# Decayed linear attention and two gated MLPs on one core: transposing a chunk's q and k together, by 64-row halves of the array

## The chip, the cores and the metric

One core of a Trainium2 chip. The metric is the device time of one execution in microseconds (us), the median over runs. Engine names are those of the profile: PE is the matrix engine, PEld its weight loads, DVE, ACT and POOL the vector, scalar and GpSimd engines, SP the engine that issues the loads.

## What is computed

The reference, cut to what matters. Attention runs over blocks with a state that decays; its output goes through a gated MLP, and that one's output through a second MLP with h·cos(h).

```python
for b in range(nb):                       # q, k, v: (2, 8, 768, 64), blocks of 64
    intra = einsum('bhic,bhjc->bhij', qb, kb) * Dmask
    intra = einsum('bhij,bhjd->bhid', intra, vb)
    inter = einsum('bhid,bhde->bhie', qb * lam_pow, kv_state)
    out[:, :, sl] = intra + inter
    kv_state = lam_block * kv_state + einsum('bhsd,bhse->bhde', kb * rev_pow, vb)
x = out as (1536, 512)
g = x @ w_gate; x = (silu(g) * (x @ w_val)) @ w_out      # inner width 1536
h = x @ w_in;   y = (h * cos(h)) @ w2_out                # inner width 2048
```

## The kernel before

Attention is done in 12 chunks of 128 tokens (6 for each batch), all 8 heads at once, in fp32. A chunk takes these steps on PE; the letters are those of the table `STEPS`, which sets their order by hand:

- `q`, `k` (line 1072): four transposes each, of 128 tokens by two heads (128 columns), into one PSUM bank; `q` against `anti`, which reverses the tokens, `k` against `ident`. ACT copies each bank to SBUF (`t_copy_job`, tiles `qt` and `kt`, 128x512).
- `s` (line 1089): scores, 8 matmuls that each use 64 rows of the array, the two halves writing two banks. DVE multiplies them with the decay mask (`at`).
- `a` (line 1102): scores by `v`, 8 matmuls with 64 output columns each. `c` (line 1111) adds the state's part on four 64x64 quarters. ACT and DVE then split the sum into two parts for the MLP (`xh`, `xl`).
- `d` (line 1096): the state's update from `kd` (made on POOL) and `v`.
- `m`, once: 16 small matmuls that write the mask.
- `u`: one unit of the first MLP, 12 matmuls of 512 columns (lines 154 to 156), put between steps of attention. Units need the outputs of four chunks.

A suffix is the chunk: `a6` is step `a` of chunk 6. An fp32 matmul is two rows of the profile (x16 for 8 matmuls), a transpose is one.

A second table, `LOADS`, sets the order in which SP issues the loads of q, k, v (one of 256 KB per chunk each) and of the first weights (`G0` and so on, two loads each); tiles come from pools of 3, 3 and 5 buffers (`BUFS`). While the program is built, a planner walks both tables with costs per step (`ATT_NS`, `SWITCH`, the landing rules in `qkv_job`), and so fixes the order of all other work: which matmul of the MLPs comes next, the order on ACT, DVE and POOL. Where it reckons that PE would stand idle for over a microsecond in attention, it puts matmuls on zeros there (`zero`, 256 columns of bf16), as many as fill the gap.

When attention is over its tiles are freed (`open_mlp`), and the rest of the program is the two MLPs: 2568 matmuls.

Of the kernel before, what the change touches and what calls it, by code (L numbers as in the profile page):

```python
# [13 lines left out]
ALU = mybir.AluOpType  # L14
# [33 lines left out]
EARLY = 4  # L48
LATENCY = 130
ISSUE = 400  # L50
STALL, FETCHES = 1000, (13300, 20600, 28400, 36000, 44000, 51500, 62500)
BEHIND = 7000
ATT_NS = {"t": 437, "mask": 700, "s": 892, "st": 464, "av": 875, "qs": 440}
TILES = {"mask": "32", "s": "64*128", "st": "128*64", "av": "128*64", "qs": "64*64"}
STEPS = (
# [3 lines left out]
)  # L59
LOADS = (  # L60
    "q0 k0 k1 q1 k2 q2 v0 k3 k4 q3 k6 v1 q4 q5 q6 k5 v2 v3 k7 v4 q7 v5 G0 v6 q8 v7 "
    "k8 v8 q9 k9 q10 q11 k10 V0 k11 v9 v10 v11 G1 V1"
)
HELD = 6, 7, 8, 9
BUFS = {"q": 3, "k": 3, "v": 5, "qt": 2, "kt": 2, "qd": 3, "kd": 2, "at": 2, "stmp": 2}
WARM = 4, 5


# [4 lines left out]
def kernel(  # L73
# [152 lines left out]

    def att_tile(nm, i):

        shape = {"q": [P, H, D], "k": [P, H, D], "v": [P, H, D], "kd": [P, H, D], "at": [P, H, C], "stmp": [P, NPAIR, D]}
        return att.tile(shape.get(nm, [P, NPAIR, C]), F32, tag=f"{nm}{i}", name=nm)  # L230

    def zero(ps, n):
# [52 lines left out]
            xs[nm, blk] = tuple(xp.tile([P, KD, TB], F32R, tag=f"{t}{blk}", name=t) for t in ("xh", "xl"))  # L285
        return xs[nm, blk]

    kinds = {"q": ("t", "q"), "k": ("t", "k"), "m": ("mask",), "s": ("s",), "d": ("st",), "a": ("av",), "c": ("qs",)}
    steps_of = [None if o == "u" else kinds[o[0]] + ((int(o[1:]),) if o[1:] else ()) for o in STEPS.split()]


# [212 lines left out]
    def signal(name, t):  # L504

        when[name] = t
        for job in blocked.pop(name, ()):
            resume(job, t)
# [93 lines left out]

        return "plain2" in when and ("r", 0, "3") not in when

    last_small, last_tiles = [False], [None]

    def switch(sub):

        kind = sub["op"][0]
        return SWITCH.get(kind, 110) if TILES.get(kind) != last_tiles[0] else 0  # L610

    def small(sub):

# [27 lines left out]
    def run_pe(sub, end, idle):  # L641

        unit = any(sub is s for s in pe_units)
        last_small[0] = small(sub)
        last_tiles[0] = TILES.get(sub["op"][0])
        for subs in (pe_att, pe_units, pe_downs):
            subs[:] = [s for s in subs if s is not sub]
        items = []
        for _ in range(int(sub["bank"])):
            item = min(stock["bank"])  # L650
            stock["bank"].remove(item)
            items.append(item[1])
            if unit:
                unit_banks.add(item[1])
        sub["fn"](*(items or [None]), **({"idle": idle} if idle and sub["op"][0] in ATT_NS and items else {}))
        for key in sub["keys"]:
            left[key] -= 1
            if not left[key]:
                give("ring", where.pop(key), end)
                ring_down(end)  # L660
        sub["then"](end + LATENCY)

    def drop_bank(i, t):

        unit_banks.discard(i)
        give("bank", i, t)
# [260 lines left out]
    def qkv_job(nm, g):  # L927

        src = {"q": q, "k": k, "v": v}[nm]
        i = yield "take", nm  # L930
        t = att_tile(nm, i)
        b, c = divmod(g, CPB)
        made_att[nm, g] = i, t
        yield go("SP", 1100, lambda: nc.sync.dma_start(t, src[b, :, c * C:(c + 1) * C, :].rearrange("h p d -> p h d")))  # L934
        signal((nm, g), landing((yield "now",) - LATENCY - 1100 + 3000, 1140))

    def mask_job(got):

# [6 lines left out]
            drop_bank(b, (yield "now",))  # L945
        signal("dmask", (yield "now",))

    def t_copy_job(nm, g, b, ps):

        i = yield "take", nm + "t"  # L950
        t = att_tile(nm + "t", i)
        yield act(t.rearrange("p a i -> p (a i)"), ps, AF.Copy)
        made_att[nm + "t", g] = i, t
        drop_bank(b, (yield "now",))
        signal((nm + "t", g), (yield "now",))
        if nm == "q" and g % CPB:
            yield "wait", "lrow"
            j = yield "take", "qd"
            qd = att_tile("qd", j)
            yield tt(qd[:, :, ::-1], t, lrow, ALU.mult, "POOL")  # L960
            made_att["qd", g] = j, qd
            signal(("qd", g), (yield "now",))
            done("qt", g, (yield "now",))

    def kd_job(g):

# [11 lines left out]
    def done(nm, g, t):  # L978

        n = readers[nm, g] = readers.get((nm, g), 0) + 1  # L980
        if n == (2 if nm in ("k", "v", "qt") and (nm == "qt" and g % CPB or nm != "qt" and g % CPB != CPB - 1) else 1):
            give(nm, made_att.pop((nm, g))[0], t)

    def tmp_job(g):
# [65 lines left out]
    def att_sub(op):  # L1050
# [1 line left out]
        kind, g = op[0], op[-1]  # L1052
        got = []
        needs, n = {
            "t": lambda: ([op[1:]], 1), "mask": lambda: (["skewed"], 4), "s": lambda: ([("qt", g), ("kt", g)], 2),
            "st": lambda: ([("kd", g), ("v", g)], 1), "av": lambda: ([("at", g), ("v", g)], 2),
            "qs": lambda: ([("av", g), ("state", g), ("qd", g)], 0),
        }[kind]()
# [5 lines left out]
        def fn(*bs, idle=0):  # L1064
            got.extend((b, bank_tile(b)) for b in bs if b is not None)
            if got:
                ps = got[0][1]
                zero(ps, idle)
            if kind == "t":
                src = made_att[op[1], g][1]  # L1070
                for p in range(NPAIR):
                    nc.tensor.transpose(  # L1072
                        ps[:, p * P:(p + 1) * P], src[:, 2 * p:2 * p + 2, :].rearrange("p a d -> p (a d)"),
                        anti if op[1] == "q" else ident,
                    )
            elif kind == "mask":
                for a in range(P // QB):
                    for r, (_, ps) in enumerate(got):
                        rows = slice(QB * r, QB * r + QB)
                        nc.tensor.matmul(  # L1080
                            ps[QB * a:QB * a + QB, 0:2 * C].rearrange("p (g x) -> p g x", g=2), ident[rows, rows],
                            skewed[1][rows, :, QB * a:QB * a + C], start=True, stop=True, tile_position=(QB * r, QB * a),
                        )
            elif kind == "s":
                qt, kt = made_att["qt", g][1], made_att["kt", g][1]
                for p in range(NPAIR):
                    for h2, (_, ps) in enumerate(got):
                        r = slice(64 * h2, 64 * h2 + 64)
                        nc.tensor.matmul(ps[:, p * C:(p + 1) * C], kt[r, p, :], qt[r, p, :], start=True, stop=True)  # L1089
            elif kind == "st":  # L1090
                pv = ps[:, 0:NPAIR * D].rearrange("p (a e) -> p a e", a=NPAIR)
                kd, vn = made_att["kd", g][1], made_att["v", g][1]
                for p in range(NPAIR):
                    for h2 in range(2):
                        h = 2 * p + h2
                        nc.tensor.matmul(pv[64 * h2:64 * h2 + 64, p, :], kd[:, h, :], vn[:, h, :], start=True, stop=True)  # L1096
            elif kind == "av":
                at_, vn = made_att["at", g][1], made_att["v", g][1]
                made_att["out", g] = list(got)
                for f in range(2):  # L1100
                    for a in (0, 2, 1, 3):
                        nc.tensor.matmul(  # L1102
                            put(got, f, a), vn[:, 2 * a + f, :], at_[:, 2 * a + f, :],
                            start=a % 2 == 0, stop=not g % CPB and a % 2 == 1, skip_group_check=True,
                        )
            else:
                out_, qd = made_att["out", g], made_att["qd", g][1]
                for y in range(2):
                    for f, a in ((0, y), (1, y + 2), (0, y + 2), (1, y)):
                        r = slice(64 * f, 64 * f + 64)  # L1110
                        nc.tensor.matmul(  # L1111
                            put(out_, f, a), state[g % 2][r, a, :], qd[r, a, :], start=False, stop=y == 1, skip_group_check=True
                        )

        def then(t):
            if kind == "t":
                spawn(t_copy_job(op[1], g, *got[0]), seen[op] + 1, t)
                done(op[1], g, t)
            elif kind == "mask":
                spawn(mask_job(got), seen[op], t)  # L1120
            elif kind == "s":
                spawn(at_job(g, got), seen[op] + 1, t)
                done("qt", g, t)
                done("kt", g, t)
            elif kind == "st":
                spawn(state_job(g, *got[0]), seen[op], t)
                done("kd", g, t)
# [527 lines left out]
```

## Time and profile before

| | |
|---|---|
| median of 3 runs | 587.58 us (587.55 to 587.71) |
| the profiled execution's own time | 587.25 us |
| its span | 585.5 us |
| PE busy | 579.5 us, 99% of the span |
| DVE, ACT, POOL busy | 504.5, 363.8, 33.4 us |
| chain that ended last | PE 97%, DMA 2% |
| attention on PE | 4.18 to 72.30 us of the span, with six units in it |

The span runs from the first to the last instruction of the program; the execution's own time is 1.75 us longer. An engine's busy share says little where it overlaps with others: what ends the program is read from the chain and from the waits.

### The profile page before, as it was taken

The numbers are of one execution on the slowest core, as the hardware profiler recorded it, in microseconds if no ns is written. First come the engines' busy times: TensorE is split into PE (matmuls) and PEld (weight loads), VectorE is DVE, ScalarE is ACT, GpSimd is POOL, SyncE is SP. The second block draws the span as 40 slices with busy tenths as digits, with TensorE's granted clock in tenths as the row PEclk, the third lists the DMA queues.
The fourth block names the chain that finished last, engine by engine and source line by source line (L and its number), as shares of the span: only waits on it lengthen the run. The fifth ranks groups of instructions, "written<-read, shape, count | busy, mean of one in ns | idle before, by whom it ended". The sixth has DMA issues, their size and how long they took to land.

```text
span 585.5 us, 9450 instructions
## 1 busy us (share of the span) xinstructions
PE 579.5 (99%) x3493; PEld 491.5 (84%) x3493; DVE 504.5 (86%) x943; ACT 363.8 (62%) x689; POOL 33.4 (6%) x50
## 2 busy tenths in 40 slices
PE   8999999999999999999999999999999999999997
PEld 6888788888888888888888888888888888888886
DVE  6479799989698997797889999979898999999973
ACT  4454576777655655465443669886667676867740
POOL 6744000000000000000000000000000000000000
PEclk9999999999999999999999999999999999999999
DMA  9999523546567636426442332111202030300023
GB/s 193 213 202 213 132 61 108 163 145 186 173 195 199 182 108 178 145 90 207 136 137 80 109 125 73 58 51 37 72 32 77 1 112 34 109 0 1 1 86 132
DMA packets 72817, 66.68 MB, mean 114 GB/s; under 512 B 40002, under 2 KB 60738, under 8 KB 72770
## 3 DMA queue, kind: packets, MB, share of 16 engines
q1 hardware_dynamic: 72768, 66.07, 40.9%
q8 instruction: 27, 0.44, 0.3%
q14 instruction: 20, 0.16, 0.1%
q10 hardware_dynamic: 2, 0.00, 0.0%
HBM read 54.00 MB, written 12.06 MB: 113 GB/s over the span
## 4 chain that ended last, share of the span: by engine, by line
PE 97%; DMA 2%; SPq 0%; issue 0%; DVE 0%
PE bank L154 25%; PE bank L155 24%; PE bank L156 24%; PE bank L1485 6%; PE bank L1486 6%; PE bank L1487 6%; PE bank L1089 2%; PE bank L1072 2%; PE bank L1102 2%; DMA v<-in_v_dram 1%; PE bank L1111 1%; DMA q<-in_q_dram 1%; PE bank L1096 1%; SPq L934 0%; DVE sum L529 0%
## 5 line engine op out<-in xcount | busy, mean ns | idle before, releaser
L154 PE MATMUL bank<-xl,wh 128*128 128x512 f32 (+1 forms) x336 | 117.9, 351 | 0.0
L155 PE MATMUL bank<-xh,wh 128*128 128x512 f32 (+1 forms) x336 | 117.4, 350 | 0.0
L156 PE MATMUL bank<-xh,wl 128*128 128x512 f32 (+1 forms) x336 | 117.2, 349 | 0.0
L536 ACT ACTIVATE s<-s 128x512 f32<-128x512 f32 (+2 forms) x124 | 72.9, 593 | 54.0 <-DVE s L529 30.1
L536 ACT ACTIVATE s<-bank 128x512 f32<-128x512 f32 (+2 forms) x126 | 62.8, 501 | 62.7 <-PE bank L156 47.1
L154 PE MATMUL bank<-wl,gh 128*128 128x512 f32 (+1 forms) x196 | 75.6, 386 | 0.0
L155 PE MATMUL bank<-wh,gh 128*128 128x512 f32 (+1 forms) x196 | 75.6, 386 | 0.0
L156 PE MATMUL bank<-wh,gl 128*128 128x512 f32 (+1 forms) x196 | 75.4, 385 | 0.0
L536 ACT ACTIVATE gh<-s 128x512 fp32r<-128x512 f32 x84 | 52.7, 629 | 36.0 <-PE bank L1486 22.3
L529 DVE TENSOR_TENSOR sum<-bank,sum 128x512 f32<-128x512 f32 (+1 forms) x97 | 62.8, 679 | 11.0 <-PE bank L156 8.2
L154 PEld LDWEIGHTS bank<-xl,wh 128*128 128x128 f32 x336 | 63.5, 189 | 9.5 <-issue 0.3
L156 PEld LDWEIGHTS bank<-xh,wl 128*128 128x128 f32 x336 | 63.5, 189 | 8.6 <-DVE wl L541 0.2
L155 PEld LDWEIGHTS bank<-xh,wh 128*128 128x128 f32 x336 | 63.6, 189 | 8.4
L529 DVE TENSOR_TENSOR s<-bank,s 128x512 f32<-128x512 f32 (+1 forms) x102 | 56.8, 561 | 15.3 <-PE bank L156 14.0
L536 ACT ACTIVATE wh<-ct 128x512 fp32r<-128x512 f32 x91 | 55.8, 625 | 17.1 <-DVE ct L205 12.4
L541 DVE TENSOR_TENSOR wl<-ct,wh 128x512 fp32r<-128x512 f32 x91 | 61.7, 685 | 4.1 <-ACT wh L536 3.8
L529 DVE TENSOR_TENSOR gl<-s,gh 128x512 fp32r<-128x512 f32 x84 | 57.4, 686 | 5.2 <-ACT gh L536 4.9
L1486 PE MATMUL bank<-gh,wh 128*128 128x512 f32 x144 | 56.1, 390 | 0.0
L1485 PE MATMUL bank<-gh,wl 128*128 128x512 f32 x144 | 56.1, 390 | 0.0
L1487 PE MATMUL bank<-gl,wh 128*128 128x512 f32 x144 | 56.0, 389 | 0.0
L205 DVE SCALAR_TENSOR_TENSOR ct<-ct,raw 128x512 int32<-128x512 int32 x68 | 48.1, 707 | 2.8 <-ACT ct L193 1.2
L193 ACT ACTIVATE ct<-raw 128x512 f32<-128x512 f32 x68 | 44.5, 662 | 3.8 <-DMA raw<-in_moe_w_in_dram 1.9
(170 smaller groups left out, 1029.8 us busy)
## 6 DMA issues: line engine op xcount, KB each, us to landing
raw<-in_moe_w_out_dram SPq DMA_DIRECT2D x28, 512.0 KB, 3.4
raw<-in_moe_w_in_dram SPq DMA_DIRECT2D x16, 512.0 KB, 3.9
raw<-in_moe_w_gate_dram SPq DMA_DIRECT2D x24, 256.0 KB, 4.7
raw<-in_moe_w_val_dram SPq DMA_DIRECT2D x24, 256.0 KB, 4.2
draftout<-raw SPq DMA_DIRECT2D x9, 512.0 KB, 2.6
q<-in_q_dram SPq DMA_DIRECT2D x12, 256.0 KB, 5.0
k<-in_k_dram SPq DMA_DIRECT2D x12, 256.0 KB, 4.9
v<-in_v_dram SPq DMA_DIRECT2D x12, 256.0 KB, 6.1
```

The lines of the kernel that those rows point to most:

```text
L154: nc.tensor.matmul(ps, wh, xl, start=first, stop=False, **kw)
L155: nc.tensor.matmul(ps, wh, xh, start=False, stop=False, **kw)
L156: nc.tensor.matmul(ps, wl, xh, start=False, stop=last, **kw)
L193: nc.scalar.activation(t, words[:, :, 1].bitcast(F32), AF.Prelu, scale=2.0 ** -112, alpha=2.0 ** 32)
L205: nc.vector.scalar_tensor_tensor(out=w, in0=w, scalar=3, in1=lo, op0=ALU.logical_shift_left, op1=ALU.bitwise_or)
L529: engine, 66 + n * 1.047 if engine == "DVE" else n * 2.45, lambda: unit.tensor_tensor(out=out, in0=in0, in1=in1, op=op),
L536: return go("ACT", (175 if fn == AF.Silu else 40) + n * 0.94, lambda: nc.scalar.activation(out, src, fn, **kw))
L541: return "any", {"DVE": 66 + n * 1.047, "POOL": n * 2.45}, lambda e: (nc.vector if e == "DVE" else nc.gpsimd).tensor_tensor(out=out, in0=i ...
L1072: nc.tensor.transpose(ps[:, p * P:(p + 1) * P], src[:, 2 * p:2 * p + 2, :].rearrange("p a d -> p (a d)"), anti if op[1] == "q" else ident,)
L1485: nc.tensor.matmul(ps, lo[:, cs], gh, start=first, stop=False)
L1486: nc.tensor.matmul(ps, hi[:, cs], gh, start=False, stop=False)
L1487: nc.tensor.matmul(ps, hi[:, cs], gl, start=False, stop=last)
```

## The change

`q` and `k` of a chunk become one step `t`. Each transpose of 128 tokens is cut into two, one for each half of the tokens: 64 rows of the array, 64 columns of `ident` or `anti`, 128 columns of weights. The upper half's results go to one bank and the lower half's to another, q and k side by side in each, so that a step takes two banks. ACT empties them with two copies of 512 columns into one tile `qkt`. The loads are in another order, the steps too, with three units among them in place of six, and the planner's costs are altered.

```diff
-ATT_NS = {"t": 437, "mask": 700, "s": 892, "st": 464, "av": 875, "qs": 440}
+ATT_NS = {"t": 470, "mask": 700, "s": 892, "st": 464, "av": 875, "qs": 440}
-TILES = {"mask": "32", "s": "64*128", "st": "128*64", "av": "128*64", "qs": "64*64"}
+TILES = {"mask": "32", "t": "64*128", "s": "64*128", "st": "128*64", "av": "128*64", "qs": "64*64"}
-    "q0 k0 m q1 k1 s0 s1 q2 k2 a0 q3 s2 a1 d0 d1 a2 c1 k3 k4 q4 c2 d2 s3 s4 q5 q6 "
+    "t0 m s0 t1 a0 t2 s1 d0 s2 d1 a1 t3 t4 a2 s3 d2 c2 c1 d3 a3 d4 c3 t5 s4 t6 s5 "
...
-    "q0 k0 k1 q1 k2 q2 v0 k3 k4 q3 k6 v1 q4 q5 q6 k5 v2 v3 k7 v4 q7 v5 G0 v6 q8 v7 "
+    "q0 k0 k1 q1 q3 k2 q4 q2 k3 q5 v0 k4 k6 k5 v1 v2 q6 k7 v3 v4 G0 v5 k8 q7 v6 q8 "
...
-    def t_copy_job(nm, g, b, ps):
+    def t_copy_job(g, got):
-        i = yield "take", nm + "t"
-        t = att_tile(nm + "t", i)
-        yield act(t.rearrange("p a i -> p (a i)"), ps, AF.Copy)
+        i = yield "take", "qkt"
+        t = att_tile("qkt", i)
+        for r, (b, ps) in enumerate(got):
+            part = t.rearrange("p a n (x i) -> p a (n x) i", x=2)[:, :, 0:4:3] if r else t.rearrange("p a n (x i) -> p a (n x) i", x=2)[:, :, 1:3]
+            yield act(part, ps.rearrange("p (n a i) -> p a n i", n=2, a=NPAIR), AF.Copy)
...
-                src = made_att[op[1], g][1]
-                for p in range(NPAIR):
-                    nc.tensor.transpose(
-                        ps[:, p * P:(p + 1) * P], src[:, 2 * p:2 * p + 2, :].rearrange("p a d -> p (a d)"),
-                        anti if op[1] == "q" else ident,
-                    )
+                for n, nm in enumerate("qk"):
+                    src = made_att[nm, g][1]
+                    for p in range(NPAIR):
+                        for h in range(2):
+                            rows, c = slice(64 * h, 64 * h + 64), h if nm == "k" else 1 - h
+                            nc.tensor.transpose(
+                                got[h][1][:, (n * NPAIR + p) * 64:(n * NPAIR + p) * 64 + 64],
+                                src[rows, 2 * p:2 * p + 2, :].rearrange("p a d -> p (a d)"),
+                                (anti if nm == "q" else ident)[rows, 64 * c:64 * c + 64],
+                            )
```

Three places show how the order moves. The first is PE from the scores of chunk 0 to its step `a0` (`at` by `v`). Before:

```order
L1089 MATMUL bank_254<-qt,kt 128x128
L1089 MATMUL bank_271<-qt,kt 128x128
L1072 MATMUL bank_287<-anti,q 128x128 x4
L1072 MATMUL bank_295<-ident,k 128x128 x4
L1102 MATMUL bank_306<-at,v 64x128 x4
```

Now, one row for each kind of matmul (bank 247 has the scores of chunk 0, banks 262 and 263 the transposes of chunk 1):

```order
L1097 MATMUL bank_247<-qkt 128x128
L1079 MATMUL bank_262<-anti,q 128x64
L1079 MATMUL bank_263<-anti,q 128x64
L1079 MATMUL bank_262<-ident,k 128x64
L234 MATMUL bank_298<-zeros 128x256
L1110 MATMUL bank_298<-at,v 64x128 x4
```

Before, PE has the scores of chunks 0 and 1 and the transposes of chunk 2 behind it when it comes to `a0`; now only the scores of chunk 0 and the transposes of chunk 1. In their place stand 26 matmuls on zeros. Five more stand ahead of the first transposes; before, the planner put none into attention.

The second place is the head of SP's queue. Before, from the fifth load on:

```order
L934 DMA k<-in_k_dram 128x8x64
L934 DMA q<-in_q_dram 128x8x64
L934 DMA v<-in_v_dram 128x8x64
L934 DMA q<-in_q_dram 128x8x64
L934 DMA v<-in_v_dram 128x8x64
```

Now:

```order
L936 DMA k<-in_k_dram 128x8x64
L936 DMA q<-in_q_dram 128x8x64 x2
L936 DMA v<-in_v_dram 128x8x64 x2
L936 DMA q<-in_q_dram 128x8x64
L936 DMA k<-in_k_dram 128x8x64 x2
```

The first `v` was the seventh load and is the eighth; q of chunk 3 goes ahead of it. Further down, v of chunk 6 is the 25th load in both.

The third place is PE around `a6` (bank 786 of the new order has its result). Now:

```order
L1119 MATMUL bank_727<-qd,state_97 64x128
L1079 MATMUL bank_761<-anti,q 128x64
L1079 MATMUL bank_762<-ident,k 128x64
L1110 MATMUL bank_786<-at,v 64x128 x4
L1104 MATMUL bank_805<-v,kd 64x64 x8
L154 MATMUL bank_819<-xl,wh 128x512
L1097 MATMUL bank_857<-qkt 128x128
```

Before, the scores of chunk 7 and the state's update with chunk 6, `s7` and `d6`, stood ahead of `a6`; now both come behind it, `s7` behind the first unit too.

## Rows read from the trace of the kernel before

**Rows 1.** The page's first part: busy time, share of the span, instructions.

```profile
PE 579.5 (99%) x3493; PEld 491.5 (84%) x3493; DVE 504.5 (86%) x943; ACT 363.8 (62%) x689; POOL 33.4 (6%) x50
```

**Rows 2.** Waits of PE over the whole span: us in total, times, longest.

```profile
PE bank L234 <- DVE halfpi L1594: 1.1, 1, 1.1
PE bank L1102 <- DMA v<-in_v_dram: 0.5, 1, 0.5
PE bank L1072 <- DMA q<-in_q_dram: 0.4, 1, 0.4
```

**Rows 3.** Timeline of PE, start of attention: start us, us, matmuls merged.

```profile
11.91 1.09 PE L1102 MATMUL bank<-at,v 128*64 128x128 f32 x16
12.94 0.66 PE L1072 MATMUL bank<-anti,q 128*128 128x128 f32 x4
13.52 1.16 PE L1089 MATMUL bank<-qt,kt 64*128 64x128 f32 x16
```

**Rows 4.** Timeline of PE, further on, for the pace of each step.

```profile
25.07 1.04 PE L1102 MATMUL bank<-at,v 128*64 128x128 f32 x16
25.95 0.63 PE L1096 MATMUL bank<-v,kd 128*64 128x64 f32 x16
26.41 1.04 PE L1102 MATMUL bank<-at,v 128*64 128x128 f32 x16
...
51.49 0.60 PE L1072 MATMUL bank<-anti,q 128*128 128x128 f32 x4
51.93 0.60 PE L1072 MATMUL bank<-ident,k 128*128 128x128 f32 x4
52.46 2.08 PE L1089 MATMUL bank<-qt,kt 64*128 64x128 f32 x32
54.47 0.67 PE L1111 MATMUL bank<-qd,state 64*64 64x128 f32 x16
```

**Rows 5.** Weight loads by form, 10 to 75 us: busy us, mean ns of one.

```profile
L1102 PEld LDWEIGHTS bank<-at,v 128*64 128x64 f32 x192 | 10.3, 137 | 1.8 <-issue 1.5 <-DVE at L529 0.2
L1089 PEld LDWEIGHTS bank<-qt,kt 64*128 64x128 f32 x174 | 10.3, 187 | 0.9 <-issue 0.5 <-ACT kt L536 0.2 <-ACT xh L536 0.2
L1096 PEld LDWEIGHTS bank<-v,kd 128*64 128x64 f32 x160 | 5.6, 137 | 1.1 <-issue 0.9 <-POOL kd L529 0.2
L1072 PEld LDWEIGHTS bank<-ident,k 128*128 128x128 f32 x40 | 4.5, 140 | 0.8 <-issue 0.5
```

**Rows 6.** Timeline of PE from step a6 to the end of attention.

```profile
35.98 1.07 PE L1102 MATMUL bank<-at,v 128*64 128x128 f32 x16
36.98 0.66 PE L1072 MATMUL bank<-anti,q 128*128 128x128 f32 x4
37.57 0.47 PE L154 MATMUL bank<-xl,wh 128*128 128x512 f32 x1
...
40.49 0.60 PE L1072 MATMUL bank<-ident,k 128*128 128x128 f32 x4
...
71.70 0.67 PE L1111 MATMUL bank<-qd,state 64*64 64x128 f32 x16
72.30 0.50 PE L154 MATMUL bank<-xl,wh 128*128 128x512 f32 x1
```

**Rows 7.** The same, in the MLP: the thirteenth matmul after a start at 79.23.

```profile
79.23 0.39 PE L154 MATMUL bank<-xl,wh 128*128 128x512 f32 x1
...
81.95 0.39 PE L154 MATMUL bank<-xl,wh 128*128 128x512 f32 x1
```

**Rows 8.** SP's queue: issue of the seventh load (v0) and the 25th (v6).

```profile
6.12 1.15 SPq L934 DMA_DIRECT2D v<-in_v_dram  x1
...
27.94 1.28 SPq L934 DMA_DIRECT2D v<-in_v_dram  x1
```

**Rows 9.** Issues at 6.12 (at 8.50 alike) and at 27.94: KB, us to landing.

```profile
v<-in_v_dram SPq DMA_DIRECT2D x1, 256.0 KB, 5.1
...
v<-in_v_dram SPq DMA_DIRECT2D x1, 256.0 KB, 7.4
```

More of the change, by code (lines that the diff above doesn't have):

```diff
@@ L50 @@
 ISSUE = 400
-STALL, FETCHES = 1000, (13300, 20600, 28400, 36000, 44000, 51500, 62500)
+STALL, FETCHES = 1000, (13000, 20600, 29000, 36500, 45000, 54500, 63500)
 BEHIND = 7000
-ATT_NS = {"t": 437, "mask": 700, "s": 892, "st": 464, "av": 875, "qs": 440}
-TILES = {"mask": "32", "s": "64*128", "st": "128*64", "av": "128*64", "qs": "64*64"}
+ATT_NS = {"t": 470, "mask": 700, "s": 892, "st": 464, "av": 875, "qs": 440}
+TILES = {"mask": "32", "t": "64*128", "s": "64*128", "st": "128*64", "av": "128*64", "qs": "64*64"}
 STEPS = (
[3 rows of a table removed]
[3 rows of a table added]
 )
 LOADS = (
-    "q0 k0 k1 q1 k2 q2 v0 k3 k4 q3 k6 v1 q4 q5 q6 k5 v2 v3 k7 v4 q7 v5 G0 v6 q8 v7 "
-    "k8 v8 q9 k9 q10 q11 k10 V0 k11 v9 v10 v11 G1 V1"
+    "q0 k0 k1 q1 q3 k2 q4 q2 k3 q5 v0 k4 k6 k5 v1 v2 q6 k7 v3 v4 G0 v5 k8 q7 v6 q8 "
+    "v8 v7 k9 q9 q10 k10 k11 q11 V0 v9 v11 v10 V1 G1"
 )
 HELD = 6, 7, 8, 9
-BUFS = {"q": 3, "k": 3, "v": 5, "qt": 2, "kt": 2, "qd": 3, "kd": 2, "at": 2, "stmp": 2}
+BUFS = {"q": 3, "k": 3, "v": 5, "qkt": 2, "qd": 3, "kd": 2, "at": 2, "stmp": 2}
 WARM = 4, 5
@@ L227, in att_tile @@
     def att_tile(nm, i):
-        shape = {"q": [P, H, D], "k": [P, H, D], "v": [P, H, D], "kd": [P, H, D], "at": [P, H, C], "stmp": [P, NPAIR, D]}
+        shape = {"q": [P, H, D], "k": [P, H, D], "v": [P, H, D], "kd": [P, H, D], "at": [P, H, C], "stmp": [P, NPAIR, D], "qkt": [P, NPAIR, 2, C]}
         return att.tile(shape.get(nm, [P, NPAIR, C]), F32, tag=f"{nm}{i}", name=nm)
@@ L286, in x_tiles @@
         return xs[nm, blk]
-    kinds = {"q": ("t", "q"), "k": ("t", "k"), "m": ("mask",), "s": ("s",), "d": ("st",), "a": ("av",), "c": ("qs",)}
+    kinds = {"t": ("t",), "m": ("mask",), "s": ("s",), "d": ("st",), "a": ("av",), "c": ("qs",)}
     steps_of = [None if o == "u" else kinds[o[0]] + ((int(o[1:]),) if o[1:] else ()) for o in STEPS.split()]
@@ L603, in turning @@
         return "plain2" in when and ("r", 0, "3") not in when
-    last_small, last_tiles = [False], [None]
+    last_small, last_tiles = [False], [None, True]
     def switch(sub):
         kind = sub["op"][0]
-        return SWITCH.get(kind, 110) if TILES.get(kind) != last_tiles[0] else 0
+        if TILES.get(kind) != last_tiles[0]:
+            return SWITCH.get(kind, 145)
+        return 60 if last_tiles[1] and kind not in ATT_NS else 0
     def small(sub):
@@ L644, in run_pe @@
         last_small[0] = small(sub)
-        last_tiles[0] = TILES.get(sub["op"][0])
+        last_tiles[:] = TILES.get(sub["op"][0]), sub["op"][0] in ATT_NS
         for subs in (pe_att, pe_units, pe_downs):
@@ L934, in qkv_job @@
         yield go("SP", 1100, lambda: nc.sync.dma_start(t, src[b, :, c * C:(c + 1) * C, :].rearrange("h p d -> p h d")))
-        signal((nm, g), landing((yield "now",) - LATENCY - 1100 + 3000, 1140))
+        signal((nm, g), landing((yield "now",) - LATENCY - 1100 + 3000, 1200 if landed[0] < 15000 else 1130))
     def mask_job(got):
@@ L946, in mask_job @@
         signal("dmask", (yield "now",))
-    def t_copy_job(nm, g, b, ps):
-        i = yield "take", nm + "t"
-        t = att_tile(nm + "t", i)
-        yield act(t.rearrange("p a i -> p (a i)"), ps, AF.Copy)
[L953 to L956, printed above, removed]
+    def t_copy_job(g, got):
[4 more added lines that the diff above has]
+            yield act(part, ps.rearrange("p (n a i) -> p a n i", n=2, a=NPAIR), AF.Copy)
+            drop_bank(b, (yield "now",))
+        made_att["qkt", g] = i, t
+        signal(("qkt", g), (yield "now",))
+        if g % CPB:
             yield "wait", "lrow"
@@ L959, in t_copy_job @@
             qd = att_tile("qd", j)
-            yield tt(qd[:, :, ::-1], t, lrow, ALU.mult, "POOL")
+            yield tt(qd[:, :, ::-1], t[:, :, 0], lrow, ALU.mult, "POOL")
             made_att["qd", g] = j, qd
             signal(("qd", g), (yield "now",))
-            done("qt", g, (yield "now",))
+            done("qkt", g, (yield "now",))
     def kd_job(g):
@@ L980, in done @@
         n = readers[nm, g] = readers.get((nm, g), 0) + 1
-        if n == (2 if nm in ("k", "v", "qt") and (nm == "qt" and g % CPB or nm != "qt" and g % CPB != CPB - 1) else 1):
+        if n == (2 if nm in ("k", "v", "qkt") and (nm == "qkt" and g % CPB or nm != "qkt" and g % CPB != CPB - 1) else 1):
             give(nm, made_att.pop((nm, g))[0], t)
@@ L1054, in att_sub @@
         needs, n = {
-            "t": lambda: ([op[1:]], 1), "mask": lambda: (["skewed"], 4), "s": lambda: ([("qt", g), ("kt", g)], 2),
+            "t": lambda: ([("q", g), ("k", g)], 2), "mask": lambda: (["skewed"], 4), "s": lambda: ([("qkt", g)], 2),
             "st": lambda: ([("kd", g), ("v", g)], 1), "av": lambda: ([("at", g), ("v", g)], 2),
@@ L1084, in fn @@
             elif kind == "s":
-                qt, kt = made_att["qt", g][1], made_att["kt", g][1]
+                qt, kt = (made_att["qkt", g][1][:, :, n] for n in range(2))
                 for p in range(NPAIR):
@@ L1116, in then @@
             if kind == "t":
-                spawn(t_copy_job(op[1], g, *got[0]), seen[op] + 1, t)
-                done(op[1], g, t)
+                spawn(t_copy_job(g, got), seen[op] + 1, t)
+                done("q", g, t)
+                done("k", g, t)
             elif kind == "mask":
@@ L1122, in then @@
                 spawn(at_job(g, got), seen[op] + 1, t)
-                done("qt", g, t)
-                done("kt", g, t)
+                done("qkt", g, t)
             elif kind == "st":
```

4 rows, old and new, of the table STEPS are left out of this document.

## Prediction

> **What bounds the kernel now.** Read the first part of the page: PE is busy 99% of the span [rows 1]. That share alone proves little, so read PE's waits next: in the whole span it waits three times, 2.0 us in all, for the first tile to be set, for a load of q and for one of v [rows 2]. Otherwise it never waits, to the end of attention and through both MLPs, and the timeline shows an even pace there: twelve matmuls of 512 columns in 2.72 us, 79.23 to 81.95 [rows 7]. So matrix work taken out of the program shortens it one for one, unless a wait opens in its place. DVE, at 504.5 us, is next, and far enough off for a shift of some us.
>
> A second limit lies close behind PE in attention: the loads. v of chunk 6 is the 25th load, issued at 27.94 and landed 7.4 us later, at 35.3 [rows 8, 9]. Step a6, which reads it, starts at 35.98 [rows 6]. PE uses it 0.6 us after it can. A faster PE runs into this landing.
>
> **What is removed: transposes.** Four transposes between other transposes take 0.44 us (51.49 to 51.93), 0.11 each [rows 4], so q and k of a chunk 0.87. The new step has 16 transposes of 64 columns, in eight pairs whose members use different halves of the array. No row shows one. Bounds: step d moves 64 columns in pairs and takes 0.46 us for eight pairs (25.95 to 26.41), 57 ns a pair; step s also works in 64-row halves, moves 128 columns, and takes 2.01 us for 16 pairs with one change of shape in it, some 112 ns a pair [rows 4]. If the two halves did not overlap at all, 16 times 57 would make the same 112 ns a pair. So a step costs 0.46 to 0.90 us against 0.87 now: a gain of 0.41, or a loss of 0.03.
>
> Which end is nearer is read from the weight loads. Each pair needs two loads of 128 columns. In s such a load lasts 187 ns; with 64 columns, in a and d, 137; but in the transposes, with 128 columns, only 140 [rows 5]. A transpose's weights are loaded as fast as half as many ordinary ones. The new step thus resembles d in both parts: loads of about 140 ns, 64 columns moved. s shows that loads into the two row halves overlap: two of 187 ns in every 112 ns. I take 57 ns a pair.
>
> Against this stands a rule of the Trainium skill (TensorE: Matmul & The Clock Gate, LDWEIGHTS): a weight load takes its columns divided by 1.2 GHz, whatever its rows. By it 128 columns take 107 ns in the new step too, and nothing is gained on PE. The 50 ns between 187 and 137 agree with it (64 columns by the rule: 53 ns); the 140 of the transposes do not.
>
> **Changes of shape.** Each change of the array's shape costs about 0.15 us: four transposes between a and s take 0.58 (12.94 to 13.52), 0.14 over their own 0.44 [rows 3]. t has now the shape of s. Four transposes between a and a unit of their own shape take 0.59 all the same (36.98 to 37.57) [rows 6], so going from transposes to matmuls may cost something without a change of shape: 0 to 0.1 us for each t before an s, I take half.
>
> **The start.** t0 needs k0 as well as q0 and the first transposes come 1.2 us later. That costs nothing in the end, since a0 waits for v0: it was the seventh load, issued at 6.12, landing 5.1 us later, and is now the eighth, halfway to the load issued at 8.50 that also takes 5.1 [rows 8, 9]: 12.4. The order shows that PE has then done two transposes, the mask and one set of scores, less than before, and the 26 matmuls on zeros fill the gap; by themselves they cost nothing as long as they end before v0 lands. a0 starts at 12.5 instead of 11.91 [rows 3]. On SP q3, now ahead of v0, waits for t0 to free its buffer; that holds v0 back by less than a place in the queue.
>
> **From a0 to a6.** In the new order there are six steps a, six t, six s, five d and five c between. One a is 0.88 (25.07 to 25.95), s 0.90, d 0.46 [rows 4], c 0.60 less one change, 0.44 (71.70 to 72.30) [rows 6]: 5.3 + 2.7 + 5.4 + 2.3 + 2.2 = 17.9. With 18 changes of shape at 0.16, 2.9, PE would reach a6 at 12.5 + 20.8 = 33.3. The bytes ahead of v6 are the same, so v6 lands at 35.3, and a6 starts at 35.5 whatever was won before. The 2 us between are waits: at a6 itself, and before it where steps wait for ACT's copies (s2 for a second copy that stands behind four others) or for v5 and q7. This is the late thing that takes the place of the saved work. The gain so far: 35.98 - 35.5 = 0.5.
>
> **From a6 on.** Before, 36.3 us to the start of the pure MLP (35.98 to 72.30) [rows 6]. Now s7 and d6 come behind a6: +0.90 + 0.46 = +1.4. Four chunks' transposes remain: 4 x 0.41 = -1.7. Changes of shape fall from 19 to 17: -0.3. A unit amid attention takes 2.92 (37.57 to 40.49), in the MLP 2.72 [rows 6, 7]; three move there, and most of the 0.2 is already in the changes: -0.2. Two steps t before an s: +0.1. Together -0.7. ACT copies as much as before, two copies of 512 columns a chunk; POOL reads one tile for another: nothing, as long as no step waits for them, and from a6 on the loads and copies run ahead of PE by 0.7 us or more in this walk. The MLPs have the same matmuls, in a partly different order; with no wait in 510 us before [rows 2] I take none now; should DVE fall behind there, each wait adds in full.
>
> **The sum.** -0.5 - 0.7 = -1.2 us. The profiled execution took 587.25, so 586.05; the median stands 0.33 higher, so **586.4**. A measurement of this kernel tells about 0.2% from no change, 1.2 us: the forecast lies on that edge.
>
> **Rivals.**
>
> *The halves don't run at 57 ns a pair (slower).* At 112 ns the step costs 0.90. The loads' slack then vanishes: six steps add 2.6 to the 20.8, a6 starts at 35.9 to 36.4, 0 to 0.4 behind now, and the four later chunks gain nothing (-1.7 becomes +0.1). The sum: +0.2 + 1.1 = +1.3, and up to +2 with the second price of a t before s: 588.9 to 589.6. It needs over about 95 ns a pair to turn the sign (1.2 us over 32 later pairs is 38 ns). For it: s, the only rows with 64-row tiles, has 112. Against it: those are bound by 128 moved columns as well, and the weights of transposes load in 140. Serial halves, the change not doing what it says, end here too.
>
> *The loads don't hold a6 (faster).* If the queue runs 1 to 2 us ahead of its present rhythm, because buffers come free sooner or fewer stalls fall on it, a6 starts up to 2 us earlier: -2 to -3, 584.6 to 585.6. Against: the bytes are the same, and the landings now follow each other at the queue's own pace.
>
> *More waits (no change).* The steps between a6 and a9 have 0.7 us of slack on q9 and q11 by the same walk. A queue that is later by 1 us, through SP's waits for buffers that are now freed in another order, adds about that: 587.0 to 588.0.
>
> **How the numbers follow.** The forecast's case 0.60, of which half lies beyond 0.2% (0.31 faster, 0.27 no change, 0.02 slower). Pairs not at 57 ns: 0.16, slower, with 0.02 of no change in between. Loads earlier: 0.13, faster. More waits: 0.11, split 0.06 no change, 0.04 slower, 0.01 faster. Together 0.45 faster, 0.35 no change, 0.20 slower. The range takes in the early loads' nearer part and reaches to the low end of the slower rival: 584.9 to 588.8.
>
> **What would show it.** PE's starts in line 1079: pairs 57 ns apart, a chunk's 16 within 0.5 us; 112 would prove the first rival. The start of a6's matmuls: near 35.5 with a wait for v just before it; 33 to 34 would prove the second. PE's waits should total 2 to 3 us more than now, all before 36 us. The pure MLP should begin near 62.9 us (35.5 + 36.3 - 0.7, less three units of 2.72). A wait of PE in the MLPs, or a start of the pure MLP above 64, would make the forecast wrong.

## The result, and the profile after

The changed kernel takes 592.04 us (median of 6 runs, 590.59 to 594.37) against 587.64 (6 runs, 587.36 to 588.50): 1.0079 times as long, with a 95% interval of 1.0064 to 1.0093 (given below in brackets). The change is slower by 4.4 us; the prediction said 586.4, and 584.9 to 588.8. The profiled execution is the fastest of the six, 590.59 with a span of 588.8 (before: 585.5).

Of the page, the first part answers to [rows 1]:

```profile
PE 578.5 (98%) x3620; PEld 491.8 (84%) x3620; DVE 506.0 (86%) x943; ACT 362.5 (62%) x689; POOL 34.1 (6%) x50
```

PE is busy 1.0 us less than before, in a span that is 3.3 us longer. The 31 added matmuls on zeros count as busy too (the 26 ahead of `a0` take 3.0 us), so the useful matrix work shrank by more than 1.0 us, and idleness came in. PE's waits over the whole span (us in total, times, longest) show where; they answer to [rows 2]:

```profile
PE bank L154 <- ACT s L536: 3.0, 2, 2.9
PE bank L1110 <- DMA v<-in_v_dram: 1.5, 1, 1.5
PE bank L1097 <- ACT qkt L536: 1.2, 3, 0.6
PE bank L234 <- DVE halfpi L1602: 1.1, 1, 1.1
PE bank L1088 <- DVE skewed L269: 0.2, 1, 0.2
```

The second, third and fifth stand in attention or right ahead of it; the fourth was there before. The first is new, and lies in the MLPs, where before PE never waited. PE's timeline (start us, us) shows its larger part:

```profile
514.64 0.28 PE L155 MATMUL bank<-w3h,wh 128*128 128x256 f32 x1
514.76 0.28 PE L156 MATMUL bank<-w3h,wl 128*128 128x256 f32 x1
517.90 0.50 PE L154 MATMUL bank<-xl,wh 128*128 128x512 f32 x1 [2.86 <-ACT s L536]
518.24 0.40 PE L155 MATMUL bank<-xh,wh 128*128 128x512 f32 x1
```

Between 514.76 and 517.90 no matmul starts; 0.12 us is the usual distance there. The step at 517.90 adds to a bank whose first contents ACT must have copied out. ACT's timeline:

```profile
515.31 0.61 ACT L536 ACTIVATE gh<-s 128x512 fp32r<-128x512 f32 x1
516.74 0.63 ACT L536 ACTIVATE gh<-s 128x512 fp32r<-128x512 f32 x1 [0.81 <-DVE s L529]
517.27 0.58 ACT L536 ACTIVATE s<-bank 128x512 f32<-128x512 f32 x1
```

The copy `s<-bank` stands behind a `gh<-s`, and that one waits 0.81 us for DVE. DVE's timeline over the same stretch has no gap:

```profile
514.37 1.13 DVE L529 TENSOR_TENSOR s<-bank,s 128x512 f32<-128x512 f32 x2
515.42 0.68 DVE L541 TENSOR_TENSOR wl<-ct,wh 128x512 fp32r<-128x512 f32 x1
516.02 0.68 DVE L529 TENSOR_TENSOR s<-s 128x512 f32<-128x512 f32 x1
516.62 0.69 DVE L529 TENSOR_TENSOR gl<-s,gh 128x512 fp32r<-128x512 f32 x1
```

So a full queue of DVE holds ACT, ACT's order holds the copy, and the copy holds PE. The small part of this wait is at 336 us:

```profile
335.44 0.39 PE L156 MATMUL bank<-xh,wl 128*128 128x512 f32 x1
336.00 0.50 PE L154 MATMUL bank<-xl,wh 128*128 128x512 f32 x1 [0.16 <-ACT s L536]
336.34 0.40 PE L155 MATMUL bank<-xh,wh 128*128 128x512 f32 x1
```

The idle time is 0.16 us. From start to start it is 0.56 us where 0.23 is usual, so PE comes 0.3 us later by it.

Attention, PE's timeline, with [rows 3], [rows 4] and [rows 6] to compare:

```profile
9.16 3.01 PE L234 MATMUL bank<-zeros 128*128 128x256 bf16 x26
13.62 1.09 PE L1110 MATMUL bank<-at,v 128*64 128x128 f32 x16 [1.45 <-DMA v<-in_v_dram]
...
36.31 1.09 PE L1110 MATMUL bank<-at,v 128*64 128x128 f32 x16
...
44.33 0.46 PE L1079 MATMUL bank<-anti,q 64*128 64x64 f32 x8
44.63 0.41 PE L1079 MATMUL bank<-ident,k 64*128 64x64 f32 x8
44.88 1.11 PE L1097 MATMUL bank<-qkt 64*128 64x128 f32 x16
...
63.77 0.50 PE L154 MATMUL bank<-xl,wh 128*128 128x512 f32 x1
```

A chunk's 16 transposes take 0.55 us (44.33 to 44.88), boundaries included, where two groups of four with theirs took 1.0 to 1.2. The step a6 begins at 36.31 instead of 35.98, 0.33 later; from a6 to the pure MLP it takes 27.46 us, and with three more units to do there (3 x 2.72) 35.6, against 36.3 before: 0.7 less. In this profile attention as a whole gained 0.4 us, and the MLPs lost the span's 3.3 and this 0.4, 3.7. In a second profile of the same kernel (e10) the pure MLP, the part behind attention, began at 64.54 instead of 63.77, so a gain of 0.4 is less than what two executions differ by.

### The profile page after: what moved, and what is told of

Read it like the earlier page. It is cut to its first block, busy times and chain, and to the rows that moved or that the text cites. A ratio compares the mean times of both kernels' runs of the same rounds, so it can differ in the third digit from the quotient of the medians.

```text
span 588.8 us, 9643 instructions
## 1 busy us (share of the span) xinstructions
PE 578.5 (98%) x3620; PEld 491.8 (84%) x3620; DVE 506.0 (86%) x943; ACT 362.5 (62%) x689; POOL 34.1 (6%) x50
## 4 chain that ended last, share of the span: by engine, by line
PE 84%; DVE 11%; ACT 2%; DMA 1%; issue 1%; SPq 0%; ACTq 0%; DVEq 0%
PE bank L154 21%; PE bank L155 21%; PE bank L156 20%; PE bank L1493 5%; PE bank L1494 5%; PE bank L1495 5%; DVE s L529 2%; DVE sum L529 2%; PE bank L1110 2%; PE bank L1097 2%; DVE wl L541 1%; DMA v<-in_v_dram 1%; PE bank L1119 1%; PE bank L1079 1%; PE bank L1104 1%; DVE s L1241 1%
## 5 line engine op out<-in xcount | busy, mean ns | idle before, releaser
L529 DVE TENSOR_TENSOR s<-bank,s 128x256 f32<-128x256 f32 (+1 forms) x102 | 57.3, 563 | 22.2 <-PE bank L156 21.3
L205 DVE SCALAR_TENSOR_TENSOR ct<-ct,raw 128x512 int32<-128x512 int32 x68 | 46.4, 689 | 3.1 <-ACT ct L193 1.3
```

The costliest lines, as they stand in the source:

```text
L205: nc.vector.scalar_tensor_tensor(out=w, in0=w, scalar=3, in1=lo, op0=ALU.logical_shift_left, op1=ALU.bitwise_or)
L529: engine, 66 + n * 1.047 if engine == "DVE" else n * 2.45, lambda: unit.tensor_tensor(out=out, in0=in0, in1=in1, op=op),
```

## Experiments

Theory A: the change set the planner's whole order of the MLPs anew, and that order has a step behind a full DVE queue; the transposes are innocent. Its rivals: B, PE comes sooner and meets DVE's bound in any order; C, the loss is in the attention.

### The order of the MLPs: e1, e2, e5

e1 puts three units back into the change's attention, six as before:

```diff
-    "s11 c9 u d10 a10 a11 c10 c11"
+    "s11 c9 u d10 u a10 u a11 u c10 c11"
```

> The changed kernel with three of the MLP's units put back into the attention part (d10 u a10 u a11 u c10 c11 in place of d10 a10 a11 c10 c11: six units there as before, where the change left three). Transposes, loads and the other steps stay. Theory A (order of the MLP): with another count of units ahead, the planner sets the MLP's steps in another order; the change's order makes TensorE wait 0.3 us near 335 and 2.9 us near 515 for banks behind a full VectorE queue, and with six units that wait goes: 588.0 to 589.0 us, no spacing over 1 us after the attention. Theory B (TensorE simply comes to VectorE's bound sooner, whatever the order): about 3 us of waits stay somewhere in the MLP, 591 to 592.5. Theory C (the loss is in the attention, by the transposes, the zeros or the waits for v): nothing changes beyond 0.5 us, 591.5 to 592.5.

Measured: 588.58 us (588.22 to 588.94, 11 runs), 1.0022 times the kernel before [1.0013, 1.0031]. After 64 us PE's list of waits is empty, though all transposes are still the change's. A's forecast holds, and C falls for the larger part of the loss. What stays is 0.2%, 1.3 us; the pure MLP begins at 73.05 here, against 72.30 before. B is not tested by this run: with six units behind it PE starts the pure MLP 1.1 us later than the change would with three more units (63.77 and 3 x 2.72).

e2 is the counterpart, the kernel before with three of its six units moved behind the attention:

```diff
-    "s8 s9 u q10 a8 k10 q11 k11 s10 s11 c8 a9 a10 d9 u d10 u a11 c10 c9 u u c11"
+    "s8 s9 u q10 a8 k10 q11 k11 s10 s11 c8 a9 a10 d9 u d10 a11 c10 c9 c11"
```

> The kernel before with three of its six units taken out of the attention part (d10 a11 c10 c9 c11 in place of d10 u a11 c10 c9 u u c11), so that they come after it; transposes, loads and the order otherwise as before. Theory A: it gets the change's order of the MLP and with it a wait of about 3 us near 515 to 520: 591 to 592 us with nothing of the change's transposes. Theory B: pure MLP work begins near 64.5 us, so the same 3 us. Theory C: within 0.5 us of the kernel before, 587.2 to 588.2, as neither transposes nor loads changed.

Measured: 591.57 us, 1.0077 [1.0061, 1.0092]: the change's loss without any of its transposes or loads. PE's waits and timeline in this kernel:

```profile
PE bank L152 <- ACT s L534: 2.9, 1, 2.9
```

```profile
515.40 0.28 PE L154 MATMUL bank<-w3h,wl 128*128 128x256 f32 x1
518.55 0.50 PE L152 MATMUL bank<-xl,wh 128*128 128x512 f32 x1 [2.87 <-ACT s L534]
```

It is the same wait, before the same kind of step, for the same copy. (A wait of 0.7 us for the state, at the end of attention, is new here too.)

e5 leaves the change's attention as it is, and its three units, and moves only the later order:

```diff
-EARLY = 4
+EARLY = 8
```

> The changed kernel with one number of the planner altered, EARLY 8 in place of 4: the jobs that turn a finished tile into the next MLP's input are due eight units ahead instead of four. The attention part and the first 250 us or so of the MLP stay instruction for instruction; only the later order changes. Theory A (the order of the MLP): the 2.9 us wait near 515 goes although TensorE begins the MLP at the same moment, 63.8 us, with the same three units ahead: 588.2 to 589.0 us; the small wait near 335 stays, and perhaps one of 0.5 to 1 us near 380. Theory B (coming early costs whatever the order): 590.5 to 592. If the clock falls only behind long waits, its runs lie within 1 us of each other, where those of the change spread over 3.8 us.

Measured: 588.08 us (587.83 to 588.85, 11 runs), 1.0014 [1.0005, 1.0023]. The pure MLP begins at 63.87, as in the change, so B falls by this run alone: PE comes as early and loses 2.4 us less in the profile (span 586.4 against 588.8). What is left of listed waits from 64 us on stands at 383 us:

```profile
PE bank L156 <- DVE gl L529: 0.4, 1, 0.4
```

### The parts alone: e3, e4

e3 has the change's order of steps and loads and the planner's landing times for it, with the transposes, copies and buffers of before (`q0 k0` where the change has `t0`, and so on); e4 has the new transposes in the old order and loads (`t0` where the later of `q0` and `k0` stood, the earlier left out).

> The change's order of steps and of loads with the transposes, copies and buffers of the kernel before (q g and k g in a row where the change has t g). The attention will end some 4 us later than with the change, as two copies follow each pair of transposes and the scores wait for both. Theory A: the MLP's order is almost the change's, so the wait near 515 to 520 stays near 3 us although TensorE comes to it 4 us later: 594.5 to 596. Theory B: TensorE comes later, so the wait shrinks to nothing as VectorE has caught up: 591.5 to 592.5. Theory C, transposes at fault: faster than the change, under 591.

> The change's transposes, copies and buffers alone, in the order of steps and loads of the kernel before (one t g where the later of q g and k g stood). Theory A: no wait in the MLP, since six units stand in the attention, but longer waits in the attention, where a step now waits for q and k together and for both banks and a copied tile: 593 to 596 us, all of the loss before 80 us. Theory B: the MLP begins later, no wait there, the same. Theory C: the transposes cost more than before even here; TensorE's time in the transposes' lines would be over 0.87 us a chunk.

Measured: e3 596.86 us (595.24 to 598.25), 1.0161 [1.0145, 1.0178]; e4 595.24 (594.99 to 595.41), 1.0134 [1.0120, 1.0148]. In e3 the pure MLP begins at 68.00, 4.2 us later than with the change, and PE meets the wait from 518.98 to 522.12, as long as ever (2.9): coming later does not shorten it. Its median lies over the expected range. Its run at a granted clock of 1.000 took 595.24, inside the range; the other three, at 0.991 to 0.997, lie above it, and the next part is about that. e4 has no wait after the attention, which ends at 80.31, 8.0 us later than before. So in the new order the new transposes are worth 4.2 us, in the old one they cost 8.0: steps and transposes can't be judged apart.

### The spread of the runs: e9, e10

In e3's profile PE ran at half pace behind the wait. Stretches of that profile: us, busy us of PE, PEld, DVE, ACT and POOL with counts, then PEclk, the granted clock as a share of the full one; below it two rows of PE's timeline:

```profile
519.00:522.00 3.00, 0.26 (x3) 0.05 (x1) 2.98 (x6) 2.19 (x6) 0.00 (x0) 1.00 0.00 0
522.00:527.00 5.00, 4.88 (x14) 3.88 (x15) 3.64 (x7) 3.30 (x6) 0.00 (x0) 0.66 0.00 0
```

```profile
523.07 0.63 PE L153 MATMUL bank<-xh,wl 128*128 128x512 f32 x1
523.50 0.63 PE L151 MATMUL bank<-xl,wh 128*128 128x512 f32 x1
```

After 2.9 us of idleness PE's matmuls of 512 columns started 427 ns apart, from 522.6 to 525.6, instead of 227: 1.2 of 2.4 GHz. That costs 1.5 us on top of the wait. e9 fills the change's wait with work on zeros, added to an accumulation that is open anyway; e10 is the change itself beside it.

```diff
+            if op == ("r", "d", 12):
+                keep = list(acc.values())[0][1]
+                for _ in range(46):
+                    nc.tensor.matmul(keep[:, 0:128], fill, fill, start=False, stop=False, skip_group_check=True)
```

> The change as it is, with 46 matmuls on zeros (128 columns, added to an accumulation that is open anyway) put ahead of the step that waits near 515, so that TensorE works through most of the wait. Nothing else moves; the wait's end is still set by ScalarE's copy. If the spread of the change's runs (590.6 to 594.4 us) comes from TensorE's clock falling behind the 2.9 us of idleness: every run between 590.3 and 591.2, granted clock 0.999 or more, and the median 1 to 1.5 us under that of the change run beside it. If the spread has another cause, or the zeros end long before the copy: the same spread as the change. If the zeros end later than the copy: up to 1 us is added to all runs.

> The change itself, unaltered, on the chip and beside the runs of the version with the filled wait: median 591.5 to 592.5 us, spread over 3 us, as measured already. With more runs it shows whether each run's granted clock goes with its time: 0.999 to 1.000 for those under 591.3, 0.998 or less for those above, at about 0.6 us for each 0.001 (half clock over 0.002 of 590 us makes 1.2 us of which half is lost).

Measured: e9 591.78 us, all five runs within 591.51 and 592.09, granted clock 0.999 or 1.000; e10 592.94, its four runs 591.38 (clock 1.000), 592.49 (0.997), 593.40 and 593.69 (0.994). The times go with the clock, and the spread is gone where PE has work. e9's median is 1.2 us under e10's, as expected, but 0.6 us over the upper end of its own range; in its profile the attention ended at 65.30, 1.5 us later than in the change's first profile (64.54 in e10's). That the clock fell behind the wait in the slower runs of the change itself is concluded from this: both of its profiles are of runs at 0.999 or more, and only e3's trace shows the fall. PE's timeline of e9 shows the filled wait:

```profile
516.37 2.74 PE L1308 MATMUL bank<-fill 128*128 128x128 bf16 x46
519.39 0.50 PE L155 MATMUL bank<-xl,wh 128*128 128x512 f32 x1 [0.28 <-ACT s L537]
```

### The price of a transpose: e8

In e1's version every transpose is made twice.

```diff
-                    for p in range(NPAIR):
+                    for p in sorted([0, 1, 2, 3] * 2):
```

> The six-unit version (588.58 us) with every transpose of a chunk made twice over into the same place: 16 more in each of the 12 t steps, the same result. At 57 ns a pair a step gains 0.46 us. If TensorE's own work sets the whole attention after a0 (ten steps t2 to t11 behind it, less the 1.2 us of waits for copies): 3.4 to 4.6 us more, 592 to 593.2. If loads hold a6, only the four steps behind it count: 1.8 to 2.3 us more, 590.4 to 590.9. At 112 ns a pair (halves one after the other) 0.9 a step: 595.5 or more.

Measured: 592.22 us (592.12 to 592.36), 3.6 us more than e1. PE's timeline of e8 around chunk 6:

```profile
31.05 0.65 PE L1077 MATMUL bank<-anti,q 64*128 64x64 f32 x16
31.54 0.66 PE L1077 MATMUL bank<-ident,k 64*128 64x64 f32 x16
32.04 1.11 PE L1095 MATMUL bank<-qkt 64*128 64x128 f32 x16
...
38.40 1.09 PE L1108 MATMUL bank<-at,v 128*64 128x128 f32 x16
```

Sixteen pairs take 0.99 us (31.05 to 32.04), 62 ns a pair, so one set 0.5. The 3.6 us lie in the range given for PE's own work behind a0 (3.4 to 4.6), and not in that for loads that hold a6 (1.8 to 2.3). Of the eight sets ahead of a6, some 4 us, a6 shows half: 38.40 against 36.44 in e1. The other half went mostly into waits that were there anyway: the one for v sank from 1.9 to 0.7, and one of 0.6 for a copy, ahead of s5, is gone. The four sets behind a6 show in full: the pure MLP begins at 77.02 against 73.05, 2.0 beyond a6's 1.96.

### What holds a6: e7, e11

Both move v0 ahead of q4, q2, k3 and q5 in the loads of e1's version; on SP's queue it then is the sixth load instead of the eighth. e11 also leaves out the zeros.

```diff
-    "q0 k0 k1 q1 q3 k2 q4 q2 k3 q5 v0 k4 k6 k5 v1 v2 q6 k7 v3 v4 G0 v5 k8 q7 v6 q8 "
+    "q0 k0 k1 q1 q3 k2 v0 q4 q2 k3 q5 k4 k6 k5 v1 v2 q6 k7 v3 v4 G0 v5 k8 q7 v6 q8 "
...
-ZERO, ZERO_FROM = 115, 1000
+ZERO, ZERO_FROM = 115, 100000
```

> The six-unit version (588.58 us) with v0 moved four places forward in the loads, ahead of q4, q2, k3 and q5. It lands about 1 to 2 us sooner, and a0 starts as much sooner than 13.75. If TensorE's own work sets a6 (a late a0 carries through): a6 1 us or more sooner than 36.44 and 587.3 to 587.8 us. If the loads and copies between hold a6 where it is: a0 sooner, a6 within 0.3 us of 36.4, the gained time comes back as waits for copies or loads between 15 and 36 us, and 588.3 to 588.9.

> The six-unit version with v0 four places forward (588.28 us), now without matmuls on zeros in the attention: the 15 ahead of a0 and the 14 ahead of a2 go, and so do the five ahead of the first transposes. In that version a0 came 1.1 us sooner and a6 not at all; 14 zeros stood for 1.6 us right ahead of a2, while the third v landed at 20.4 and a2 began at 21.7. If the zeros took the time (they end after what they wait for): a0 near 11 to 11.5, a2 near 20.4 to 20.6, a6 near 35.4 to 35.8, 587.2 to 587.7 us. If loads and copies hold a6: a2 perhaps sooner, a6 within 0.3 us of 36.5, 588.0 to 588.6. If the clock falls in the gaps that the zeros filled: matmuls at half pace somewhere before 36 us, and 588.6 or more.

Measured: e7 588.28 us (588.10 to 589.70), 1.0017 [1.0009, 1.0026], not told apart from e1. a0 begins at 12.61, 1.1 us sooner than in e1, and a6 at 36.56, 0.1 later. PE's timeline of e7:

```profile
7.40 2.08 PE L1094 MATMUL bank<-qkt 64*128 64x128 f32 x16
9.27 0.64 PE L1076 MATMUL bank<-anti,q 64*128 64x64 f32 x8
...
20.08 1.70 PE L231 MATMUL bank<-zeros 128*128 128x256 bf16 x14
21.71 1.09 PE L1107 MATMUL bank<-at,v 128*64 128x128 f32 x16
```

The 1.1 us are lost right ahead of a2, where 14 matmuls on zeros stand: a2 begins at 21.71, against 21.13 in e1. PE waits for no load of q, k or v in this profile.

e11: 587.22 us (587.01 to 588.44), 0.9999 [0.9990, 1.0008]. This is 1.4 us under e1 and lies in the range given for the zeros (587.2 to 587.7), not in that for loads and copies (588.0 to 588.6). The profile is of an execution of 587.98 us at clock 0.997. In it a0 begins at 10.31, 3.4 us sooner than in e1, and a6 at 36.23, only 0.2 sooner:

```profile
10.31 1.35 PE L1107 MATMUL bank<-at,v 128*64 128x128 f32 x16
13.61 0.69 PE L1076 MATMUL bank<-anti,q 64*128 64x64 f32 x8 [1.96 <-DMA q<-in_q_dram]
14.06 0.67 PE L1076 MATMUL bank<-ident,k 64*128 64x64 f32 x8
14.49 2.05 PE L1094 MATMUL bank<-qkt 64*128 64x128 f32 x16
16.47 0.91 PE L1101 MATMUL bank<-v,kd 128*64 128x64 f32 x16
```

```profile
14.50:16.50 2.00, 2.00 (x23) 1.78 (x20) 0.00 (x0) 1.70 (x6) 0.00 (x0) 0.50 0.94 208
```

Here t2 waits 1.96 us for the q that v0 overtook, and behind this gap the granted clock is 0.50 and the scores take 1.98 us (14.49 to 16.47), where without it they take 1.04. So in these two profiles what is won at a0 is taken back by the next load, by zeros that last longer than the wait that they stand for, or by the clock.

Neither profile refutes that a late a0 carries through: behind t2 and up to a6 PE waits for no load in either, and six of e11's runs, at a clock of 1.000, took 587.01 to 587.22. With e8 this speaks for PE's own work behind a0 as what sets a6. It isn't settled, as no trace of one of those six runs was taken.

### Versions without the wait: e6, e12

e6 is the change with five units ahead (`d10 a10 a11 u u c10 c11`), EARLY 6 and MARGIN 200; a1 comes behind t3, and v0, k5, k8, k10 and q8 are moved by one to three places in the loads. e12 is e6 with a1 ahead of t3 again, v0 ahead of q4, and no zeros in the attention.

> A version meant to have no wait in the MLP and little of the attention's loss: the change with five units ahead in place of three (two more before the last c10 c11), EARLY 6, MARGIN 200, a1 one step later, and v0, k5, k8, k10, q8 moved by one to three places in the loads. Theory A: no wait after the attention, 586.7 to 587.5, the kernel before or a little under. Theory B: 590 or more. A result between 588 and 589 would say that the loss in the attention, not the wait, decides here.

> The five-unit version without a wait in the MLP (587.34 us), with v0 ahead of q4, a1 back in its place ahead of t3, and without zeros in the attention. If zeros and v0 were what kept a6 at 36.3: 586.2 to 586.7, under the kernel before by 0.1 to 0.2%. If a6 is held by loads and copies: 587.1 to 587.5, no difference.

Measured: e6 587.34 us, 0.9999 [0.9990, 1.0008], no difference from the kernel before, and no wait after the attention. e12: 586.82 (585.86 to 588.00, 11 runs) beside 587.57 of the kernel before in the same series, 0.9987 [0.9979, 0.9996]. It is under the kernel before by about 0.7 us, or 0.13%, a difference too small to build on. Its two runs at a clock of 1.000 took 585.86 and 586.22, the other nine, at 0.994 to 0.997, 586.65 to 588.00. The profile is one of the nine; as in e11, a gap stands in it (2.2 us for a q) with scores at half pace behind it. Its a6 begins at 36.42, so this profile doesn't show where the gain lies.

## Why the prediction was wrong

**The MLPs: the failed step.** "The MLPs have the same matmuls, in a partly different order; with no wait in 510 us before [rows 2] I take none now; should DVE fall behind there, each wait adds in full." The order was the point. Counted from start to start its two waits took 3.0 and 0.3 us, and behind each the next matmul too comes 0.1 later (517.90 to 518.24 and 336.00 to 336.34 are 0.34, where 0.23 is usual). That is 3.6 of the 3.7 us that the MLPs lost in the profile. So the condition was named, and given no chance and no price. A wait of PE in the MLPs was also the prediction's own sign of being wrong, and it came. It stood in the trace of before. The prediction read DVE's share over the span, 86% [rows 1], and called it far enough off; but the share of the stretch says otherwise. Of the kernel before:

```profile
450.00:540.00 90.00, 90.00 (x449) 76.56 (x448) 87.92 (x158) 62.55 (x113) 0.00 (x0) 1.00 0.13 43
```

DVE is busy 87.92 of 90 us there, PE all 90. There was no wait only because the order suited a queue that was 98% full. An order that is made anew doesn't have to suit it: e2 makes the loss without the transposes, e5 takes most of it away with the same attention.

**The sum.** Forecast were -0.5 up to a6, -0.7 from there on and nothing in the MLPs, -1.2 in all. The profiles have +0.3, -0.7 and +3.7, +3.3 in all.

**The clock: a term that was missing.** The median of the change lies 1.45 us over its profiled execution, that of the kernel before 0.39; the 1.1 between them turns the 3.3 us of the profiles into the 4.4 of the medians. e9 and e10 tell why: the slower runs go with a lower granted clock, and the spread goes when the wait is filled.

**From a6 on: right.** Forecast -0.7, measured 35.6 against 36.3. The total came as reckoned; of its terms only the transposes were measured by themselves.

**a6: wrong in what holds it, near by luck.** It was forecast at 35.5, held by v6, after 2 us of waits. It began at 36.31 with no wait. v6, on SP's queue and by its time to landing:

```profile
29.20 1.04 SPq L936 DMA_DIRECT2D v<-in_v_dram  x1
```

```profile
v<-in_v_dram SPq DMA_DIRECT2D x1, 256.0 KB, 5.7
```

It landed at 34.9, 1.4 us before a6, so it held nothing. a0 came late instead: forecast at 12.5, it began at 13.62, when v0 had come. v0's place in the queue was right, its landing 1.1 us off: it was issued behind q3 at 7.31, and by the end of PE's wait took some 6.2 us instead of the 5.1 of [rows 9]. From a0 to a6 it is 22.7 us: 1.2 of waits for ACT's copies and 21.5 of PE's own work, reckoned as 20.8. That saved work returns as waits was right, but they stand at a0 and at the copies.

**The transposes: right.** They take 62 ns a pair (e8), where 57 was taken, and 0.55 us a chunk with the boundaries; the bounds were 0.46 to 0.90. The rival built on 112 ns falls. Weight loads of 128 columns in them take 138 ns in the mean, as in the transposes before [rows 5]:

```profile
L1079 PEld LDWEIGHTS bank<-anti,q 64*128 64x128 f32 x80 | 3.5, 138 | 1.0 <-issue 0.9 <-ACT x L536 0.2
```

By the Trainium skill (TensorE: Matmul & The Clock Gate, LDWEIGHTS) a weight load takes its columns divided by 1.2 GHz, which makes an estimate of 107 ns for each of the two loads of a pair. Here both are done every 62 ns, so the rule doesn't give the pace of these loads into the two row halves.

**No wait for POOL or the copies from a6 on: right.** The three waits for `qkt` all stand before 36 us.

## What to carry to other kernels

Where a planner sets the order, a change of one table at the front changes the order of everything behind it. Before calling the rest "the same work", read the share of the next engine stretch by stretch, and give a new wait a price wherever it is nearly full. The order listing shows what moved.

Test such a change by moving the order alone, with the work as it was (e2, e5): that took the transposes out of suspicion at once.

## What was not expected of the hardware

Behind an idle stretch of 2.9 us in the middle of a busy program, TensorE ran at 1.2 GHz for about 3 us in e3's profile (427 ns a matmul instead of 227); in both profiles of the change, with the same idle stretch, it did not. Of the change's ten runs, four took 590.6 to 591.6 us at a clock of 0.999 or more, and six 592.5 to 594.4 at 0.994 to 0.997. Work on zeros over the idle stretch held the clock in five of five. In e11 and e12, where a gap of 2.0 and 2.2 us stands in attention without zeros, the profiles have half pace behind it.

In e7 the scores from 7.40 on took 1.87 us, to 9.27; in e1 the same ones took 0.99:

```profile
7.24 1.16 PE L1095 MATMUL bank<-qkt 64*128 64x128 f32 x16 [0.21 <-ACT qkt L534]
8.23 0.41 PE L1077 MATMUL bank<-anti,q 64*128 64x64 f32 x8
```

The spacing is nearly twice as large, and yet the granted clock reads 1.00 over this stretch of e7. Near the start of the program the distance of matmuls tells the pace, and the column doesn't. So a part of what e7 won by an earlier v0 was spent at this slower pace too.
